# Rows 8 and 9 of the first chunk's down projection as three products each, with a reordered stage around them

## The chip, the cores and the metric

The kernel runs on one core of one Trainium2 chip. The metric is the time on the device in microseconds (us) of one execution, the median over runs. The engines of the core run beside each other, each through its own list of instructions in order: TensorE (PE; PEld is its loading of weights), VectorE (DVE), ScalarE (ACT), GpSimd (POOL) and SyncE (SP), which issues the DMAs. They wait for each other through semaphores.

## The reference

An mLSTM cell over 4 batches, 8 heads, 768 steps and head size 40, and then a two-layer network with exact GELU on its output, viewed as 3072 tokens by 320 features.

```python
for t in range(S):
    m_new = np.maximum(f_gate[:, :, t] + m, i_gate[:, :, t])
    f_stab = np.exp(f_gate[:, :, t] + m - m_new)
    i_stab = np.exp(i_gate[:, :, t] - m_new)
    m = m_new
    C = f_stab * C + i_stab * (v_t outer k_t)
    n = f_stab * n + i_stab * k_t
    y[:, :, t] = sigmoid(o_gate[:, :, t]) * (C @ q_t) / max(abs(n . q_t), 1)
x = y.transpose(0, 2, 1, 3).reshape(B * S, H * D)      # 3072 x 320
h = x @ w_in                                            # w_in 320 x 2048
out = (0.5 * h * (1 + erf(h / sqrt(2)))) @ w_out        # w_out 2048 x 320
```

All inputs are float32.

## The kernel before

**Chunks.** The 768 steps are cut into 6 chunks of 128. A chunk is computed in parallel form: scores of q and k within the chunk, weighted by the gates, and the carried state for what came earlier. Its y of all 4 batches (512 tokens) is transposed to x and goes through the two matrix products: "up" to 2048 features in 16 rows of 128 and GELU, then "down", where row n of the 16 adds its product with 128 rows of w_out into the four accumulators `po`, one for each batch.

**Products.** A float32 product on TensorE shows as two records in the profile. The alternative is three products in the type fp32r: one operand is split into a rounded part `hi`, a remainder `rest` and a rounded whole `low`, the other into `w_hi` and `w_lo`, and hi with w_hi, rest with w_hi and low with w_lo are added up (`w_parts` names them). Splitting a row of GELU's output is `split_g`: two instructions on ScalarE (hi at L873, low at L875) and one on VectorE (rest at L874). Splitting rows of w_out is `out_hi` (L935, on ScalarE for rows 8 and up) and `out_lo` (L943, VectorE). In the first chunk's down projection, rows 0 to 9 are fp32 and rows 10 to 15 are three products each (`row(n)`, L888).

**Weights.** w_in and w_out come in 26 pieces (0 to 9 of w_in, 10 to 25 of w_out, so that row n of the down projection needs piece 10 + n). Each is fetched as bits (L394, a ring of four buffers) and put together again by `conv_one` (two ScalarE instructions, L404 and L405, into one of two buffers `sig` and `pow`) and `conv_two` (two VectorE instructions, L416 and L419). `conv_two` of piece i also issues the fetch of piece i + 3, into the buffer that `conv_one` of piece i - 1 has read. `conv_one` of piece i needs the buffers that `conv_two` of piece i - 2 has left.

**The order.** The first part of the kernel (chunk 0, the cell of chunk 1, and all conversions) is written out by hand as the string `FRONT`. Each word is a step, and each engine gets its instructions in that order. The words that matter here:

- `K`, `J`: the next `conv_one`, `conv_two`; K22 is that of piece 22. `F`: the next row of the first down projection.
- `G`, `Y`, `X`, `R` of batch b, for chunk 1: tanh of the output gate (L506, ScalarE); `finish`, y from the values (L685 to L690, then `y_rest` at L699, VectorE); `turn_y`, y transposed on TensorE into the PSUM tile `px` (L708) and its rounded `x_hi` on ScalarE (L718); `split_x`, `x_rest` (L727) and `x_low` (L728) on VectorE. `V` are the cell's values.
- `z`: `split_g`. `a`, `b`: `out_hi`, `out_lo` of a row (a second number is how many rows).
- `r`, `p`: halves of the gate values out to DRAM and back, swapped; `+`: copies of k and q to a scratch in DRAM; `[`: blocks of that scratch loaded; `(`, `)`: the blocks turned on VectorE; `B`: a row of M broadcast (L210, L213). All but the turning are DMAs of SyncE.

For chunk 1, `px` has two buffers: batch 2's transposes take batch 0's, batch 3's take batch 1's, once their readers are done. In chunk 1 the steps X0 and X1 also issue the loads of k and v of chunk 2 for batches 0 and 1 (`load(n + NLD, 1, 3)`), ahead of the fetches of pieces 16 and 21 in SyncE's queue. Batches 1 and 3 of the chunks from 2 on are stored with their halves swapped, so that their loads are two DMAs each (L173).

After `FRONT` comes a second string for chunk 1's up and down projections (`SECOND`); it begins with the up projection `U0`, whose products are at L966.

Of the kernel before, what the change touches and what calls it, by code (L numbers as in the profile page):

```python
# [10 lines left out]
F32R = mybir.dt.float32r  # L11
# [3 lines left out]
OP = mybir.AluOpType  # L15

P = 128
# [10 lines left out]
    g1 c1 J y1 s2 K x0 t3 x1 v2 g2 O4 J B4 g3 c2 y2 s3 B5 K x2 K L5 J T0 K v3 A y3 M1 x3 c3 G0 M0 H O7 O6 O5 J  # L28
    J i5 u0 L6 u1 K W0 J W1 I4 A K S0 T1 C0 J i6 V0 i7 u2 G2 K U M2 L7 S1 J G1 K U i8 W2 J i9 C1 T2 K
    M3 f2 S2 V1 Y0 T3 J Y1 C2 e W3 K K K J S3 J C3 f3 K X0 J K R0 J K J V2 K Y2 J J K  # L30
    K V3 X1 J K r F J K (0 )0 F J K F K J F X2 G3 F J K F Y3 R1 J K F p + + + + J F J a10,2 b10,2 z10 a12 b12 F X3 z11 F a13,3 b13,3 z12 F z13 [1 F B8 z14 F B9 R2 z15 F R3 B10 B11 F a8 b8 a9 b9 F"""
CELL = "MWGVYXRKQDCSht"

HI_AT = {3: ("w_out3", 0), 8: ("w_out3", 2), 4: ("w_out0", 0), 5: ("w_out0", 1), 6: ("w_out2", 0), 7: ("w_out2", 1), 9: ("f0", 0)}
# [22 lines left out]
def kernel(  # L57
# [16 lines left out]
    nc = tc.nc  # L74

    B, H, S, D = q.shape
# [6 lines left out]
    DM = H * D  # L83
    DFF = moe_w_in.shape[1]
    NF = DFF // P
    TG = B * L
    R = P // 2
    NX = 2
    NLD = 4
# [11 lines left out]
    two = ctx.enter_context(tc.tile_pool(name="two", bufs=2))  # L101
# [5 lines left out]
    gp = ctx.enter_context(tc.tile_pool(name="gp", bufs=1))  # L107
# [25 lines left out]
    shared = lambda shape, dt, name: wts.tile(shape, dt, name=name, tag="hi", bufs=5)  # L133
# [16 lines left out]
    def out_of(n):  # L150
        return ob[n % NLD].rearrange("p (h d) -> p h d", d=D)
# [6 lines left out]
    def swapped(c, b):  # L158

        return c > 1 and b % 2 == 1  # L160

    def load(n, first=0, end=4):

        if n >= NCH * B:
            return
        c, b = divmod(n, B)
        for src, dst in ((q, qb), (k, kb), (v, vb), (o_gate, None))[first:end]:
            if dst is kb and c > 1:
                dst = k_later
            if dst and swapped(c, b):  # L170
                x, to = src[b, :, c * L:(c + 1) * L, :].rearrange("h p d -> p h d"), dst[turn_of(n)][:, :, 0:D]
                for i in range(2):
                    nc.sync.dma_start(out=to[halves[i]], in_=x[halves[1 - i]])  # L173
                continue
            nc.sync.dma_start(out=dst[turn_of(n)][:, :, 0:D] if dst else out_of(n),
                              in_=src[b, :, c * L:(c + 1) * L, :].rearrange("h p d -> p h d"))
# [19 lines left out]
    def turn_of(n):  # L196

        return n % NLD if n < 2 * B else (n - 2 * B) % NQ
# [36 lines left out]
    a = gates.tile([BH, NCH, L], F32, name="a")  # L235
# [141 lines left out]
    def w_row(n):  # L377

        return w_rows[n // 4][:, n % 4, :]
# [50 lines left out]
    def unread(bank):  # L430
        for _ in range(idle[0]):
            nc.tensor.matmul(bank, ident, ident, start=True, stop=True, skip_group_check=True)
        idle[0] = 0
# [8 lines left out]
    def by_set(px):  # L442

        return px.rearrange("p k (a i) -> p (k a) i", a=2)

    def in_place(x, b):

        return x.rearrange("p k (a t) -> p (k a) t", a=2)[:, :, b * R:(b + 1) * R]

    def in_turns(x):  # L450

        return x.rearrange("p (a t) -> p t a", a=2)

    def in_pairs(pu):

        return pu.rearrange("p (t a) -> p t a", a=2)

    class Cell:
# [242 lines left out]
        def turn_y(self, b):  # L701
            n, t = self.c * B + b, slice(b * L, (b + 1) * L)
            pool, tag = self.side[b // 2] if self.c > 1 else (ps_tr, "tr") if self.c > 0 else (ps_mm, "b")
            px = pool.tile([P, NX + 1, L], F32, name="px", tag=tag)
            unread(px[:, 0, :])
            for k in range(NX + 1):
                y = ob[n % NLD][:, k * P:(k + 1) * P] if k < NX else self.rest.get(b, y_rest).rearrange("p two r -> p (two r)")
                nc.tensor.transpose(px[:, k, :], y, ident)  # L708
            self.turned.append(b)
            if self.c < 2 and len(self.finished) > len(self.turned):  # L710
                self.twice(b + 1)
            if self.c == 0:
                nc.scalar.copy(out=first_x[:, :, t], in_=px)
                return
            self.px[b] = px
            if "x" not in parts:
                parts["x"] = raw.tile([P, NX + 1, TG], F32R, name="x_hi", tag="x", bufs=1)
            nc.scalar.activation(out=in_place(parts["x"], b), in_=by_set(px), func=AF.Copy, scale=PART)  # L718
            if self.c == 1 and b < 2:
                load(n + NLD, 1, 3)  # L720

        def split_x(self, b):
            px = by_set(self.px.pop(b))
            if b == 0:
                parts["x_low"] = fars[0].tile([P, NX + 1, TG], F32R, name="x_low", tag="x_low", bufs=1)
            hi = in_place(parts["x"], b)
            nc.vector.tensor_tensor(out=in_place(parts["x_rest"], b), in0=px, in1=hi, op=OP.subtract)  # L727
            nc.vector.tensor_copy(out=in_place(parts["x_low"], b), in_=px)  # L728


    HF, HT = NF // 2, TG // 2

    parts, fars, w_hi, w_lo, beside = {}, [], {}, {}, []
# [118 lines left out]
    def send(c, b, o_sb):  # L852
        to = out[b * S + c * L:b * S + (c + 1) * L, :]
        if c == 0:
            nc.sync.dma_start(out=to, in_=o_sb)
            return
        for a in range(2):
            queue = nc.scalar if a and c == NCH - 1 else nc.sync
            queue.dma_start(out=to[halves[a]], in_=o_sb[a::2])

    singles, first_parts_of = [], {}

    def split_g(n):

        parts_of = []
        for i in range(3 * len(first_parts_of), 3 * len(first_parts_of) + 3):
            if i == len(singles):
                four = gp.tile([P, 4, TG], F32R, name="g_part", tag=f"g{i // 4 % 3}")
                singles.extend(four[:, j, :] for j in range(4))
            parts_of.append(singles[i])  # L870
        hi, rest, low = first_parts_of[n] = parts_of
        whole = first_g.row(n)
        nc.scalar.activation(out=hi, in_=whole, func=AF.Copy, scale=PART)  # L873
        nc.vector.tensor_tensor(out=rest, in0=whole, in1=hi, op=OP.subtract)  # L874
        nc.scalar.copy(out=low, in_=whole)  # L875

    def first_down_steps(g):
        po = []

        def row(n):  # L880

            if n == 0:
                po.extend(ps_mm.tile([P, DM], F32, name="po", tag="ab"[b // 2]) for b in range(B))
            xs, ws = ((g.row(n),), (w_row(n),)) if n not in first_parts_of else (first_parts_of[n], later.w_parts(n))
            steps = [(k, b) for k in range(len(xs)) for b in range(B)]
            for k, b in sorted(steps, key=lambda x: x[::-1]) if n == NF - 1 else steps:
                to, w = (po[b], ws[k]) if len(xs) == 1 else (in_pairs(po[b]), in_turns(ws[k]))
                nc.tensor.matmul(to, xs[k][:, b * L:(b + 1) * L], w, start=(n == 0 and k == 0),  # L888
                                 stop=(n == NF - 1 and k + 1 == len(xs)), skip_group_check=True)
                if n == NF - 1 and k + 1 == len(xs):  # L890
                    if b % 2 == 0:
                        o_sb = outp.tile([P, 2, DM], F32, name="o_sb", tag="o_sb")
                    nc.scalar.activation(out=o_sb[:, b % 2, :].rearrange("p (a i) -> p a i", a=2),
                                         in_=po[b].rearrange("p (i a) -> p a i", a=2), func=AF.Copy)
                    send(0, b, o_sb[:, b % 2, :])

        return [lambda n=n: row(n) for n in range(NF)]
# [128 lines left out]
    def in_turn(steps):  # L1026
        todo = list(steps)
        return lambda: todo.pop(0)() if todo else None
# [9 lines left out]
    def first_blocks():  # L1038
# [3 lines left out]
        for r in (32, 96):  # L1042
# [3 lines left out]
    first_g, later = Hidden(), Later()  # L1046
# [5 lines left out]
                 A=in_turn(first_up_steps(0)), U=in_turn(first_up_steps(1)), e=first_blocks, F=in_turn(first_down_steps(first_g)),  # L1052
                 K=in_turn(lambda i=i: conv_one(i) for i in n_pieces), H=products_begin,
                 J=in_turn(lambda i=i: conv_two(i) for i in n_pieces), Z=split_weight,
                 u=first_parts, f=first_pair, i=split_first, z=split_g)
    steps |= dict(a=later.out_hi, b=later.out_lo)
    cell = cell_steps(2, CELL)
    steps |= {"+": copies, "<": cell["M"], ">": cell["W"], "(": cell["K"], ")": cell["Q"],
# [5 lines left out]
    for c in range(1, NCH):  # L1064
# [3 lines left out]
                     a=later.out_hi, b=later.out_lo, E=before and before.finish,  # L1068
                     L=lambda b: n0 + b < NCH * B and load_blocks(n0 + b, by_block), B=lambda b: load_M(n0 + b),
                     j=lambda b: load(n0 + b, 1, 3), o=lambda b: load(n0 + b, 3, 4), J=lambda b: load(n0 + b + NQ, 1, 3), O=lambda b: load(n0 + b + NLD, 3, 4))  # L1070
# [37 lines left out]
```

## Time and profile before

| | |
|---|---|
| median of 3 runs | 438.4 us (438.35 to 438.49) |
| the profiled execution | 438.46 us |
| its span | 436.7 us |
| TensorE busy | 427.3 us, 98% of the span |
| TensorE weight loads | 374.6 us, 86% |
| VectorE busy | 296.0 us, 68% |
| ScalarE busy | 277.3 us, 63% |
| GpSimd busy | 48.8 us, 11% |
| granted TensorE clock | 1.0 |

A timeline row gives the start in us, the time in us to the end of the group, engine, line, operation, output and input tiles, shapes and count; in brackets is how long the engine was idle before it and what ended that. A group's time runs to the end of its last instruction, and the next one often starts a little before that, so the step from one start to the next is what an instruction costs its engine. A row of the waits gives total us, number, and the longest. For DMA rows on SyncE (SPq) the time is that of the issue, with the wait for room in the queue.

### The profile page before, as it was taken

Reading aid. Unit: us, or ns where it says so; the run is one execution under the profiler, and the core shown is the slowest. Engines: PE = TensorE matmul, PEld = TensorE weight load, DVE = VectorE, ACT = ScalarE, POOL = GpSimd, SP = SyncE. Lnnn points to the kernel's source line nnn. Section 1 sums busy time; section 2 is a strip of 40 time slices with the busy share of each in tenths; the row PEclk is TensorE's granted clock in tenths of the full one; section 3 lists DMA queues with packets and bytes.
Section 4 is the critical chain, followed back from the end, with each engine's and each line's share of the span. In section 5 each row is a group of like instructions: output and inputs, shape, how many; then the busy total and the mean of one; then the engine's idle time right before and its main releaser. Section 6 shows DMA issues by size and latency. Waiting matters only on the chain.

```text
span 436.7 us, 13291 instructions
## 1 busy us (share of the span) xinstructions
PE 427.3 (98%) x5472; PEld 374.6 (86%) x5472; DVE 296.0 (68%) x680; ACT 277.3 (63%) x595; POOL 48.8 (11%) x77
## 2 busy tenths in 40 slices
PE   8989999999999999999999999999999999999996
PEld 7777888877988899988899988899988889979986
DVE  8797687797888697747597747597746586533330
ACT  4989999856889985228785229785247715243441
POOL 3001030000430041030041030040010000000000
PEclk9999999999999999999999999999999999999999
DMA  7999994577791592662492653571561400010001
GB/s 151 220 214 243 233 256 87 138 211 179 229 154 56 106 176 60 115 179 50 84 187 42 123 158 60 117 134 32 110 156 17 62 2 2 22 42 2 1 2 60
DMA packets 162268, 48.83 MB, mean 112 GB/s; under 512 B 147776, under 2 KB 155232, under 8 KB 162208
## 3 DMA queue, kind: packets, MB, share of 16 engines
q1 hardware_dynamic: 161888, 47.65, 50.1%
q8 instruction: 43, 0.70, 0.6%
q10 hardware_dynamic: 320, 0.33, 0.2%
q14 instruction: 17, 0.14, 0.1%
HBM read 43.84 MB, written 9.37 MB: 122 GB/s over the span
## 4 chain that ended last, share of the span: by engine, by line
PE 73%; DVE 2%; ACT 2%; DMA 1%; issue 1%; ACTq 0%
PE po L991 31%; PE pu L966 24%; PE pu L977 7%; PE ps L568 3%; PE pf L621 2%; PE ph L674 1%; PE po L888 1%; PE po L674 1%; PE px L708 1%; DMA bits<-in_moe_w_out_dram 1%; PE pf L632 1%; DVE pow L416 1%; DVE w_out L419 0%; ACT w_out_part L935 0%; ACT g_part L873 0%
## 5 line engine op out<-in xcount | busy, mean ns | idle before, releaser
L991 PE MATMUL po<-w_out_part,g_parts 128*128 128x320 f32 x960 | 140.7, 303 | 0.0
L991 PEld LDWEIGHTS po<-w_out_part,g_parts 128*128 128x128 f32 x960 | 131.6, 189 | 5.9 <-issue 4.6
L986 DVE TENSOR_TENSOR g_parts<-g_whole,g_parts 128x512 fp32r<-128x512 f32 x80 | 57.0, 713 | 58.1 <-ACT g_parts L985 56.0
L984 ACT ACTIVATE g_whole<-pu 128x512 f32<-128x512 f32 x80 | 47.1, 589 | 74.2 <-PE pu L977 63.7
L985 ACT ACTIVATE g_parts<-g_whole 128x512 fp32r<-128x512 f32 x80 | 50.5, 631 | 8.3 <-PE po L991 5.1
L474 POOL TENSOR_SCALAR_AFFINE_SELECT W<-W 128x1024 f32<-128x1024 f32 (+2 forms) x20 | 21.7, 1088 | 189.2 <-DMA W<-M_d 154.4
L500 ACT ACTIVATE W<-W,aT 128x128 f32<-128x128 f32 x128 | 38.8, 389 | 0.3
L987 DVE CAST g_parts<-g_whole 128x512 fp32r<-128x512 f32 x80 | 36.2, 453 | 0.0
L699 ACT COPY far<-ob 128x128 f32<-128x128 f32 x16 | 4.6, 290 | 32.9 <-DVE ob L690 32.9
L966 PE MATMUL pu<-x_hi,w_in_hi 128*128 128x512 f32 x80 | 24.2, 384 | 0.0
L966 PE MATMUL pu<-x_hi,hi_first 128*128 128x512 f32 x80 | 24.0, 381 | 0.1
L966 PE MATMUL pu<-x_rest,hi_first 128*128 128x512 f32 x80 | 23.8, 379 | 0.0
L966 PE MATMUL pu<-x_rest,w_in_hi 128*128 128x512 f32 x80 | 23.8, 379 | 0.0
L966 PE MATMUL pu<-x_low,w_in_lo 128*128 128x512 f32 x80 | 23.8, 379 | 0.0
L966 PE MATMUL pu<-x_low,w_in 128*128 128x512 f32 x80 | 23.8, 379 | 0.0
L888 PE MATMUL po<-w_out,g 128*128 128x320 f32 x80 | 22.0, 432 | 0.0
L404 ACT ACTIVATE sig<-bits 128x320 f32<-128x320 f32 (+1 forms) x26 | 15.2, 586 | 10.4 <-issue 6.1
L574 DVE TENSOR_TENSOR W<-ps,W 128x256 f32<-128x256 f32 (+1 forms) x48 | 17.7, 414 | 4.2 <-PE ps L568 3.2
L888 PEld LDWEIGHTS po<-w_out,g 128*128 128x128 f32 x80 | 15.0, 190 | 5.9
L639 DVE TENSOR_TENSOR far<-pf,gT 128x164 f32<-128x164 f32 x32 | 8.4, 319 | 16.1 <-PE pf L632 11.7
L416 DVE SCALAR_TENSOR_TENSOR pow<-sig,pow 128x320 uint32<-128x320 uint32 (+1 forms) x26 | 15.4, 592 | 4.3 <-ACT pow L405 4.3
L1015 ACT ACTIVATE o_sb<-po 128x320 f32<-128x320 f32 x20 | 7.5, 443 | 16.7 <-PE po L991 16.7
(196 smaller groups left out, 778.9 us busy)
## 6 DMA issues: line engine op xcount, KB each, us to landing
W<-M_d SPq DMA_DIRECT2D x16, 512.0 KB, 6.5
bits<-in_moe_w_in_dram SPq DMA_DIRECT2D x20, 256.0 KB, 4.2
bits<-in_moe_w_out_dram SPq DMA_DIRECT2D x16, 320.0 KB, 4.6
blocks<-kq_d SPq DMA_DIRECT2D x32, 128.0 KB, 3.5
ob<-in_o_gate_dram SPq DMA_DIRECT2D x24, 160.0 KB, 4.1
out_dram<-o_sb SPq DMA_DIRECT2D x36, 80.0 KB, 2.0
wide<-M_d SPq DMA_DIRECT2D x4, 512.0 KB, 4.8
kq_d<-in_k_dram SPq DMA_DIRECT2D x6, 320.0 KB, 4.6
```

The lines of the kernel that those rows point to most:

```text
L416: nc.vector.scalar_tensor_tensor(out=p, in0=s, scalar=3, in1=p, op0=OP.logical_shift_left, op1=OP.bitwise_or)
L474: nc.gpsimd.affine_select(out=x, in_=x, compare_op=OP.is_ge, fill=1.0e30, base=base, pattern=[[0, H], [1, x.shape[2]]], channel_multiplier=-1)
L500: nc.scalar.activation(out=W[n][:, h, :], in_=src, func=AF.Exp, scale=-1.0, bias=aT[:, self.c, r:r + 1])
L574: nc.vector.tensor_tensor(out=w[r, :, t], in0=ps[i][hip][r, :, t], in1=w[r, :, t], op=OP.mult)
L888: nc.tensor.matmul(to, xs[k][:, b * L:(b + 1) * L], w, start=(n == 0 and k == 0), stop=(n == NF - 1 and k + 1 == len(xs)), skip_group_chec ...
L966: nc.tensor.matmul(in_pairs(pus[i][e]), w3(at[k])[n][:, e, i * P:(i + 1) * P], in_turns(x3[n][:, k, :]), start=(n == 0 and k == 0), stop=F ...
L977: nc.tensor.matmul(in_pairs(pus[i][e]), w3(r)[n][h, p % 2, i * P:(i + 1) * P], in_turns(x3[n][h, NX, :]), start=False, stop=(n == 2), skip ...
L984: nc.scalar.activation(out=whole, in_=self.pus[n // 4][n % 4 // 2][n % 2], func=AF.Gelu)
L985: nc.scalar.activation(out=hi, in_=whole, func=AF.Copy, scale=PART)
L986: nc.vector.tensor_tensor(out=rest, in0=whole, in1=hi, op=OP.subtract)
L987: nc.vector.tensor_copy(out=low, in_=whole)
L991: nc.tensor.matmul(in_pairs(self.po[t]), x[:, t * L:(t + 1) * L], in_turns(w), start=(n == 0 and k == 0), stop=(n == NF - 1 and k == 2), s ...
```

## The change

- Rows 8 and 9 of the first down projection become three products too. Their parts of g lie in three tiles from the pool's "hi" buffers, their weights' parts in four tiles with the tags "vw", "vw", "kT" and "qT" (`first_homes`).
- `split_g` is cut in two: `z` keeps the two ScalarE instructions and the new `n` (`rest_g`) does the VectorE one. The split of the weights of rows 8 and 9 is two steps as well: `h` on ScalarE, `l` on VectorE (`split_row`).
- For chunk 1, `x_low` is made by ScalarE in `turn_y`, right behind `x_hi`, instead of by VectorE in `split_x`.
- The loads of k and v of chunk 2's batches 0 and 1 leave `turn_y` and become the steps `j0 j1`, behind row 12.
- The end of `FRONT` is put in a new order: among others X3, the fourth batch's transposes, stands ahead of row 8 instead of behind it, and the two splits of g for rows 8 and 9 ahead of K23 and X2.

```diff
-    K V3 X1 J K r F J K (0 )0 F J K F K J F X2 G3 F J K F Y3 R1 J K F p + + + + J F J a10,2 b10,2 z10 a12 b12 F X3 z11 F a13,3 b13,3 z12 F z13 [1 F B8 z14 F B9 R2 z15 F R3 B10 B11 F a8 b8 a9 b9 F"""
+    K V3 X1 J K r F J K (0 )0 F J K z8 F n8 F z9 K J X2 G3 n9 h8 F J l8 K h9 F Y3 R1 l9 z10 a10,2 J K F n10 b10,2 J F p + + + + X3 z11 J a12 n11 F b12 z12 F a13,3 n12 b13,3 F z13 n13 [1 F B8 z14 n14 F j0 j1 B9 R2 z15 n15 F R3 B10 B11 F a8 b8 a9 b9 F"""
...
             nc.scalar.activation(out=in_place(parts["x"], b), in_=by_set(px), func=AF.Copy, scale=PART)
-            if self.c == 1 and b < 2:
-                load(n + NLD, 1, 3)
+            if self.c == 1:
+                if b == 0:
+                    parts["x_low"] = fars[0].tile([P, NX + 1, TG], F32R, name="x_low", tag="x_low", bufs=1)
+                nc.scalar.copy(out=in_place(parts["x_low"], b), in_=by_set(px))
...
             nc.vector.tensor_tensor(out=in_place(parts["x_rest"], b), in0=px, in1=hi, op=OP.subtract)
-            nc.vector.tensor_copy(out=in_place(parts["x_low"], b), in_=px)
+            if self.c > 1:
+                nc.vector.tensor_copy(out=in_place(parts["x_low"], b), in_=px)
...
             if i == len(singles):
-                four = gp.tile([P, 4, TG], F32R, name="g_part", tag=f"g{i // 4 % 3}")
-                singles.extend(four[:, j, :] for j in range(4))
+                n_of, at = (2, 0) if i < 6 else (4, (i - 6) // 4 % 3)
+                t = shared([P, 2, TG], F32R, "g_part") if i < 6 else gp.tile([P, 4, TG], F32R, name="g_part", tag=f"g{at}")
+                singles.extend(t[:, j, :] for j in range(n_of))
...
         nc.scalar.activation(out=hi, in_=whole, func=AF.Copy, scale=PART)
-        nc.vector.tensor_tensor(out=rest, in0=whole, in1=hi, op=OP.subtract)
         nc.scalar.copy(out=low, in_=whole)
+
+    def rest_g(n):
+
+        hi, rest, low = first_parts_of[n]
+        nc.vector.tensor_tensor(out=rest, in0=first_g.row(n), in1=hi, op=OP.subtract)
+
+    first_homes, rows_lo = [], {}
+
+    def split_row(n):
+
+        to, lo = first_homes[2 * (n - HF):2 * (n - HF) + 2]
+        later.w_hi[n], later.w_lo[n] = to, lo
+        src, to, lo = [x.rearrange(f"p ({o}) -> p a t", a=2) for x, o in ((w_row(n), "t a"), (to, "a t"), (lo, "a t"))]
+        nc.scalar.copy(out=to, in_=src)
+        return lambda: nc.vector.tensor_tensor(out=lo, in0=src, in1=to, op=OP.subtract)
...
             if n == 0:
+                first_homes.extend(two.tile([P, DM], F32R, name="w_out_part", tag=tag) for tag in ("vw", "vw", "kT", "qT"))
...
-                 u=first_parts, f=first_pair, i=split_first, z=split_g)
+                 u=first_parts, f=first_pair, i=split_first, z=split_g, h=lambda n: rows_lo.update({n: split_row(n)}), l=lambda n: rows_lo.pop(n)(), n=rest_g, j=lambda b: load(2 * B + b, 1, 3))
```

More of the change, by code (lines that the diff above doesn't have):

```diff
@@ L718, in turn_y @@
             nc.scalar.activation(out=in_place(parts["x"], b), in_=by_set(px), func=AF.Copy, scale=PART)
-            if self.c == 1 and b < 2:
-                load(n + NLD, 1, 3)
+            if self.c == 1:
+                if b == 0:
+                    parts["x_low"] = fars[0].tile([P, NX + 1, TG], F32R, name="x_low", tag="x_low", bufs=1)
+                nc.scalar.copy(out=in_place(parts["x_low"], b), in_=by_set(px))
         def split_x(self, b):
             px = by_set(self.px.pop(b))
-            if b == 0:
+            if b == 0 and self.c > 1:
                 parts["x_low"] = fars[0].tile([P, NX + 1, TG], F32R, name="x_low", tag="x_low", bufs=1)
```

## The prediction

> **What bounds the kernel now.** I read the page first (TensorE busy for 427.3 us of a 436.7 us span), then the waits of TensorE, then the timeline of each engine over 84 to 119 us, where the first chunk's down projection and the second chunk's x are made. The waits of TensorE between 80 and 170 us are one line:
>
> ```profile
> PE po L888 <- DVE g_part L874: 0.6, 2, 0.4
> ```
>
> After 118.69 us, where the second chunk's up projection starts, TensorE idles under 0.5 us, so a shift of that start is a shift of the end. TensorE's timeline of the stage:
>
> ```profile
> 85.53 8.78 PE L888 MATMUL po<-w_out,g 128*128 128x320 f32 x32
> 94.15 0.38 PE L708 MATMUL px<-ident,ob 128*128 128x128 f32 x2
> ...
> 94.47 10.93 PE L888 MATMUL po<-w_out,g 128*128 128x320 f32 x40
> 105.24 0.38 PE L708 MATMUL px<-ident,ob 128*128 128x128 f32 x2
> ...
> 105.57 2.32 PE L888 MATMUL po<-w_out,g 128*128 128x320 f32 x8
> 107.50 0.93 PE L888 MATMUL po<-w_out_part,g_part 128*128 128x320 f32 x4
> 108.70 3.53 PE L888 MATMUL po<-w_out_part,g_part 128*128 128x320 f32 x24 [0.27 <-DVE g_part L874]
> 112.61 6.24 PE L888 MATMUL po<-w_out_part,g_part 128*128 128x320 f32 x44 [0.38 <-DVE g_part L874]
> ```
>
> Four fp32 rows take 94.15 - 85.53 = 8.62, so 2.155 a row. The last 44 products take 118.69 - 112.61 = 6.08, so 0.138 each and 1.66 for a row of 12. Rows 10 to 15 should take 72 x 0.138 = 9.95 and take 118.69 - 107.50 = 11.19: 1.24 us of stall, for splits that come late. The px transposes (0.33 with what follows) never wait.
>
> VectorE's timeline: batch 0's x_rest, conversion 21's first half, Y3, and R1 behind it.
>
> ```profile
> 85.99 0.56 DVE L727 TENSOR_TENSOR x_rest<-px,x_hi 128x384 fp32r<-128x384 f32 x1 [1.07 <-ACT x_hi L718]
> 97.17 0.48 DVE L416 SCALAR_TENSOR_TENSOR pow<-sig,pow 128x320 uint32<-128x320 uint32 x1
> 101.45 0.49 DVE L685 SCALAR_TENSOR_TENSOR ob<-ob,far 128x320 f32<-128x320 f32 x1 [0.58 <-ACT ob L506]
> 103.23 0.55 DVE L727 TENSOR_TENSOR x_rest<-px,x_hi 128x384 fp32r<-128x384 f32 x1
> ```
>
> ScalarE's timeline: it waits for the bits of piece 22 (K22), then come the third batch's x_hi, the tanh of G3 that Y3 waits for, and at 106.83 row 10's split, needed at 107.50.
>
> ```profile
> 98.85 0.49 ACT L404 ACTIVATE sig<-bits 128x320 f32<-128x320 f32 x1 [1.99 <-DMA bits<-in_moe_w_out_dram]
> 100.59 0.47 ACT L718 ACTIVATE x_hi<-px 128x384 fp32r<-128x384 f32 x1
> 100.96 0.46 ACT L506 ACTIVATE ob<-ob 128x320 f32<-128x320 f32 x1
> 106.83 0.63 ACT L873 ACTIVATE g_part<-g 128x512 fp32r<-128x512 f32 x1
> ```
>
> SyncE's own queue: four k and v DMAs stand ahead of the bits of piece 21.
>
> ```profile
> 89.42 1.34 SPq L173 DMA_DIRECT2D wide<-in_k_dram  x2
> 90.86 1.27 SPq L173 DMA_DIRECT2D vb<-in_v_dram  x2
> 92.23 0.56 SPq L394 DMA_DIRECT2D bits<-in_moe_w_out_dram  x1
> ```
>
> **Part by part.** *Two rows as three products:* 2 x (2.155 - 1.66) = 0.99 us less on TensorE. The price is off it: on ScalarE four g_part operations (1.04 a row, from 108.74 to 109.77) and two weight copies (0.39); on VectorE two subtractions of 0.60 and two of 0.41. If no split came late the 1.24 of stall would go too.
>
> *x_low on ScalarE:* VectorE loses 0.47 four times (103.23 to 103.70), ScalarE gains 0.37 four times (x_hi's step, 100.59 to 100.96, the same shape). Both engines now read one px. The trace shows no two of its readers at once (x_hi, then x_rest, then x_low, each after the other); so batch 0's x_rest waits between 0 and the copy's 0.35. I take 0.35, the value by the rows, all of which stand one behind another.
>
> [...]
>
> *k and v out of the bits' queue:* SyncE issued six DMAs at the first two transposes; the four at 89.42 held piece 21 until 92.23, and the two at 78.75 held nothing that VectorE did not hold longer. Piece 22 is issued once conversion 18 has left its buffer: K18 starts 0.08 after VectorE's step 16, which moves from 90.78 to 90.66, ends 91.68, so K18 ends 92.73 and the fetch goes at 92.8. Its landing took 4.9 in the crowded queue, others 2.9 to 3.3 (issued at 78.4 and 89.0) and 4.5 (86.8). I take up to 4.4, landed by 97.2. The six DMAs now stand behind the blocks' loads and ahead of three M loads: some 3.7 us of SP issue (0.43 + 0.59, and 2.8 for the halves) ahead of B9, B10, B11. The second of these masks (L474) ran from 115.46 to 117.66 on POOL; ScalarE's weights of that batch follow 2.4 us behind 120.64, and the weighed values that POOL makes behind it (to 119.3) are read at 126.53 (L632). SP's queue runs 1 us earlier in front of them, so all this comes some 3 us later than now, to 120.7 and 122.3: still 2.3 and 4.2 us early. Uncovered, each us beyond that is a us of time. The two "vw" and one each of the "kT" and "qT" buffers that rows 8 and 9 borrow were read last by 85 us and are next written after 115 us; the same holds for the three borrowed "hi" buffers. Cost nothing.
>
> *The moved order, which decides.* The fourth px transpose goes from behind row 8 to ahead of it. It needs the second px's buffer, so batch 1's x_rest (Y3, then R1 on VectorE) must be done. TensorE is there at 85.53 + 8 x 2.155 + 0.33 = 103.1. When is R1 done? ScalarE's new copies and the two g splits now stand ahead of G3, and G3 ahead of Y3 and R1:
>
> - x_hi at 85.46, x_low to 86.31, R0 at 86.34. From R0 to the end of conversion 20, VectorE worked without a gap, 85.99 to 97.26 = 11.27; less x_low 0.47 it is 10.80: 97.14.
> - K22 needs that buffer: 97.22 (0.08, as from 87.94 to 88.02). Its bits are there. K takes 0.87; row 8's hi starts 98.09 and ends (0.62) 98.71.
> - Row 8's subtraction is now ahead of J21: 98.74 + 0.60, J21 from 99.34 to 100.36. K23 waits for J21's buffer: 100.44 (both g splits lie within that wait).
> - K23 0.87, x_hi 0.37, x_low 0.37: the tanh at 102.05, done 102.51; the weight copy of row 8 behind it 102.41 to 102.90.
> - On VectorE row 8's weight rest waits for it: 102.93 + 0.41; Y3 at 103.34, y_rest 1.64 later, R1 at 105.12 to 105.67.
> - px at 105.73, row 8 at 106.06.
>
> So TensorE waits 2.6 us at the transpose. Behind it the splits are early: row 11's rest is needed at 111.6 and done at 110.84, row 13's at 114.9 and done 114.2. No stall is left there. Eight rows of 12 x 0.138 = 13.27 end at 119.33 against 118.69: +0.64.
>
> The sum: 2.64 of new wait - 0.99 of products - 1.24 of old stall, and 0.23 in which the first product of row 10 now overlaps the last fp32 pass: +0.64. The profiled execution took 438.46 (span 436.7 and 1.8 around it), 0.06 over the median of 438.4: 439.1.
>
> **The rivals.** *No wait at the transpose (faster).* If R1 is done by 103.1, row 8 starts at 103.42 and the eight rows end at 116.69: -2.0, 436.5. For it: ScalarE has idle stretches of 2.0 and 3.0 us before 98.85 and 105.26 that the splits could fill, and VectorE is relieved. Against: filling them needs K22 and K23 2.6 us earlier, and VectorE's unbroken work from 86 us holds them. Every us by which G3 is earlier than 102.05 is a us of time; 438.75 needs only that the reads of px overlap.
>
> *Late bits (slower).* The fetch of piece 22 at 92.8 lands after 97.2, and K22, the splits, G3, Y3, R1 and the px slide with it one for one. With the 4.9 and 5.2 that the pieces issued at 93.85, 94.4 and 95.3 took it is at 97.7 to 98.0: 0.5 to 0.8 more, 439.6 to 439.9; I take 439.8. It decides slower from a landing over 4.6. For it: the halves of aT and ewT are still written through the same queue just ahead. Against: the four k and v DMAs are gone.
>
> *The move of k and v does nothing:* without those DMAs K22 is held by conversion 20 at nearly the same time, so in the forecast that part gives only what x_low and the splits take. It is in the sum.
>
> **How the numbers follow.** A measurement here tells 0.2% (0.9 us) from no change: 437.5 to 439.3. The forecast, a wait that eats the saving, has 0.58, its own range 438.6 to 439.6; 0.47 of that lies below 439.3 and 0.11 above. Late bits 0.27, no wait 0.15. So faster 0.15, same 0.47, slower 0.38. The range goes from 437.3, where 1.8 of the 2.6 us of wait are gone (G3 can come earlier by any part of it), to 440.0, the late bits' upper end: it leaves out 0.14 below and some 0.05 above.
>
> **What would show it.** Right: TensorE's row L708 with an idle of 2 to 3 us before it near 105.7, ended by VectorE's x_rest; L888 as 96 split products without an idle; K22 released by VectorE, not by a DMA; the up projection's first product near 119.3. Wrong: the transpose near 103 us without idle and the up projection near 117; or K22 ended by its DMA later than 97.4; or waits behind 120 us at the values (L632) or weights (L500) for the moved loads.

## The result and the profile after

The changed kernel took 439.97 us (median of 8 runs, 438.72 to 440.46) against 438.3 us (8 runs): a ratio of 1.0039, 95% interval 1.0027 to 1.0051. It is slower by 0.4%, about 1.7 us. The profiled execution took 439.94 us with a span of 438.1. The forecast was 439.1 and "no change that can be measured"; the time lies just under the upper end of the range, 440.0, and above the 439.3 up to which the forecast counted as no change.

TensorE's timeline of the stage, changed kernel (start, length, line, tiles; idle before it and what ended that in brackets):

```profile
85.45 8.78 PE L907 MATMUL po<-w_out,g 128*128 128x320 f32 x32
...
105.81 0.41 PE L708 MATMUL px<-ident,ob 128*128 128x128 f32 x2 [2.64 <-DVE x_rest L729]
...
106.08 14.96 PE L907 MATMUL po<-w_out_part,g_part 128*128 128x320 f32 x96
120.88 0.59 PE L985 MATMUL pu<-x_hi,hi_first 128*128 128x512 f32 x2
```

The fourth px waits 2.64 us for batch 1's x_rest; the forecast had 2.6 us at 105.73. Behind it the 96 split products (three for each fp32 product of rows 8 to 15) run without an idle, as forecast, but take 120.88 - 106.08 = 14.80 us and not 13.27. Busy times by stretch show why (columns: stretch, length, then busy time and count for TensorE, its weight loads, VectorE, ScalarE and POOL, then granted clock, DMA share and GB/s):

```profile
107.20:110.60 3.40, 3.40 (x15) 3.40 (x14) 3.33 (x7) 3.40 (x8) 0.00 (x0) 0.50 0.90 155
110.60:121.00 10.40, 10.40 (x78) 10.40 (x77) 9.61 (x15) 6.98 (x14) 3.21 (x4) 1.00 0.81 231
```

From 107.2 to 110.6 the granted clock is 0.50. TensorE is busy all of that time and does 15 products where full clock does some 25 (3.40 / 0.138). The page shows it as a single 8 in the row PEclk and nowhere else; a busy share of 98% hides it.

I call the time from row 0 of the down projection to the second chunk's up projection "the stage". It took 33.16 us before (118.69 - 85.53) and 35.43 after (120.88 - 85.45). That is +2.27 where +0.64 was worked out. The span grew by only 1.4: behind the stage the rest took 318.0 before and 317.2 after. Over all profiles of this study that rest lies between 317.1 and 318.0, and row 0 starts between 85.4 and 87.2. The two profiles of the old order have 318.0 and 317.9, those of the changed kernel and its variants 317.1 to 318.0; whether an edit moves the rest is not shown. So the stage measures the part that was edited, and the ratio of times judges the whole.

### The profile page after: what moved, and what is told of

The parts are those of the page before. It is cut to its first block, busy times and chain, and to the rows that moved or that the text cites. A ratio compares the mean times of both kernels' runs of the same rounds, so it can differ in the third digit from the quotient of the medians.

```text
span 438.1 us, 13313 instructions
## 1 busy us (share of the span) xinstructions
PE 427.8 (98%) x5480; PEld 376.6 (86%) x5480; DVE 295.6 (67%) x680; ACT 281.8 (64%) x605; POOL 48.4 (11%) x77
## 4 chain that ended last, share of the span: by engine, by line
PE 75%; DVE 1%; ACT 0%; issue 0%; DVEq 0%
PE po L1010 31%; PE pu L985 24%; PE pu L996 7%; PE po L907 3%; PE ps L568 3%; PE pf L621 2%; PE ph L674 1%; PE px L708 1%; PE po L674 1%; PE pf L632 1%; DVE ob L690 0%; DVE w_out_part L893 0%; DVE x_rest L729 0%; ACT o_sb L1034 0%; DVE ob L685 0%
## 5 line engine op out<-in xcount | busy, mean ns | idle before, releaser
L1005 DVE TENSOR_TENSOR g_parts<-g_whole,g_parts 128x512 fp32r<-128x512 f32 x80 | 57.9, 724 | 58.9 <-ACT g_parts L1004 56.7
L474 POOL TENSOR_SCALAR_AFFINE_SELECT W<-W 128x1024 f32<-128x1024 f32 (+2 forms) x20 | 20.3, 1018 | 193.9 <-DMA W<-M_d 117.3
L512 DVE STREAM_TRANSPOSE kT<-blocks 128x512 f32<-128x512 f32 x16 | 11.3, 709 | 12.3 <-DMA blocks<-kq_d 12.2
L907 PE MATMUL po<-w_out,g 128*128 128x320 f32 x64 | 17.6, 432 | 0.0
L405 ACT ACTIVATE pow<-bits,low_bits 128x320 uint32<-128x320 uint32 (+1 forms) x26 | 17.4, 669 | 0.0
```

The costliest lines, as they stand in the source:

```text
L405: nc.scalar.activation(out=p, in_=lo, func=AF.Relu, scale=0.9 * 2.0 ** -29, bias=low_bits)
L474: nc.gpsimd.affine_select(out=x, in_=x, compare_op=OP.is_ge, fill=1.0e30, base=base, pattern=[[0, H], [1, x.shape[2]]], channel_multiplier=-1)
```

## The experiments

The theory after this had two parts. **Wait theory:** the transposes moved ahead of row 8 wait for R1, which the reordered ScalarE and VectorE work makes late. **Clock theory:** the idle stretch itself halves the clock for 3.4 us and costs 1.5 more. Rivals: the added ScalarE work as such, the moved loads, the reads of px on two engines.

**Splits moved into an idle stretch of ScalarE.**

```diff
-... K J V2 K Y2 J J K
-... F J K z8 F n8 F z9 K J X2 G3 ...
+... K J V2 K z8 z9 Y2 J J K
+... F J K F n8 F K J X2 G3 ...
```

> The changed kernel with one move: the ScalarE halves of the two g splits of rows 8 and 9 stand ahead of K18, in a stretch of 1.9 us in which ScalarE idles, instead of ahead of K23. Same work, same products. Wait theory (the loss is TensorE's wait at the fourth px for batch 1's x_rest, and half a clock behind it): K23, G3, Y3 and R1 come about 1.7 us earlier, the wait falls from 2.6 to about 0.9 us, the granted clock stays 1.0, the second chunk's up projection starts near 117.5 instead of 120.9, and the time is 2.5 to 3.5 us under the changed kernel's, about 1 us under the kernel before. Work theory (the added ScalarE work itself makes the stage longer): the same work in the same stage, the up projection stays near 120 to 121 and the time within 0.5 us of the changed kernel's.

TensorE's timeline with the early splits:

```profile
86.38 8.78 PE L907 MATMUL po<-w_out,g 128*128 128x320 f32 x32
...
105.00 0.41 PE L708 MATMUL px<-ident,ob 128*128 128x128 f32 x2 [0.90 <-DVE x_rest L729]
...
105.27 13.29 PE L907 MATMUL po<-w_out_part,g_part 128*128 128x320 f32 x96
118.40 0.59 PE L985 MATMUL pu<-x_hi,hi_first 128*128 128x512 f32 x2
```

The wait is 0.90, the products take 13.13, the stage 118.40 - 86.38 = 32.02 (row 0 starts 0.9 later in this execution, so 117.5 became 118.4). The ratio to the kernel before is 0.9963 (0.9946 to 0.9980). The same work in another place turns slower into faster: the added ScalarE work as such is not the cost.

**The gap filled with products of no use.**

```diff
-... p + + + + X3 z11 ...
+... p + + + + k10 X3 z11 ...
```

> The changed kernel with ten products of no use (128x128 fp32, some 0.24 us each) on TensorE between row 7 and the fourth px: they fill 2.4 of the 2.6 us of wait and change nothing else. Clock theory (the idle stretch itself makes the clock fall to half for 3.4 us, worth 1.5 us): the transposes still come near 105.8, the granted clock is 1.0 throughout, the 96 split products take 13.3 instead of 14.8 us, the up projection starts near 119.4, and the time is about 1.5 us under the changed kernel's. Rival (the products of rows 8 to 15 run slower for another reason, as DMA or operand reads beside them, and the clock's row only goes along): the 96 products still take about 14.8 and the time stays.

TensorE's timeline with the ten fillers:

```profile
85.47 8.78 PE L907 MATMUL po<-w_out,g 128*128 128x320 f32 x32
...
103.03 2.39 PE L250 MATMUL cold<-w_out 128*128 128x128 f32 x20
105.81 0.41 PE L708 MATMUL px<-ident,ob 128*128 128x128 f32 x2 [0.39 <-DVE x_rest L729]
...
106.08 8.94 PE L907 MATMUL po<-w_out_part,g_part 128*128 128x320 f32 x64
115.23 4.61 PE L907 MATMUL po<-w_out_part,g_part 128*128 128x320 f32 x32 [0.21 <-DVE g_part L883]
119.68 0.59 PE L985 MATMUL pu<-x_hi,hi_first 128*128 128x512 f32 x2
```

The transposes come at the same 105.81, the granted clock of the profiled execution is 1.0, and the products end at 119.68 instead of 120.88. The 1.5 us expected is 1.2, because at full clock row 13's rest comes late: the products take 119.68 - 106.08 = 13.60 us, against 13.13 with the early splits. Ratio 1.0015 (0.9996 to 1.0034), no different from the kernel before. This interval overlaps that of the changed kernel, so the gain rests on the trace (a stage of 34.21 instead of 35.43) and on the clock, 0.999 or more in all 12 runs. With useless work in the gap the clock stayed up: the clock theory holds.

**The transposes moved alone, in the kernel before.**

```diff
-... z10 a12 b12 F X3 z11 F a13,3 ...
+... z10 a12 b12 X3 F z11 F a13,3 ...
```

> The kernel before with one move: the fourth px transposes ahead of row 8 instead of behind it. Wait theory: batch 1's split of x ends at 104.3 there and TensorE is at 103.1, so a wait of about 1.3 us at the transposes, ended by VectorE; it takes the place of the 1.2 us of stall at rows 10 to 12, so the up projection starts within 0.4 us of before and the time is the same within 0.5 us; a gap this short leaves the clock at 1.0. If the place of the transposes alone made the loss, the time would rise by 1.3 us or more.

```profile
105.48 0.41 PE L708 MATMUL px<-ident,ob 128*128 128x128 f32 x2 [0.76 <-DVE x_low L728]
```

That line of its TensorE timeline is the wait: 0.76 us, shorter than the 1.3 expected. The stage is 32.93, the ratio 1.0002 (0.9983 to 1.0021). The new place costs nothing by itself; it only makes R1 decisive.

**The loads of k and v back in the bits' queue.**

```diff
+                if b < 2:
+                    load(n + NLD, 1, 3)
...
-... F j0 j1 B9 R2 ...
+... F B9 R2 ...
```

> The changed kernel with the loads of k and v of chunk 2's batches 0 and 1 back at the second chunk's first two transposes. Wait theory: the bits of piece 22 land near 98.7 instead of before 97.2, everything behind K22 slides, and the wait at the fourth px grows from 2.6 to about 4.1 us: 1.0 to 2.0 us slower than the changed kernel. If the moved loads themselves cost the loss (M's masks behind them, late k and v): faster than the changed kernel by up to 1.5 us.

```profile
98.80 0.49 ACT L404 ACTIVATE sig<-bits 128x320 f32<-128x320 f32 x1 [0.41 <-DMA bits<-in_moe_w_out_dram]
```

In its ScalarE timeline K22 is again released by the bits, at 98.80; in the changed kernel it starts at 97.20. TensorE waits 3.74 us at the fourth px (4.1 expected, 2.64 in the changed kernel), the clock is at half for 6.83 us, the stage takes 37.64. Ratio 1.0061 (1.0032 to 1.0090), 1.0 us over the changed kernel by the ratios, whose intervals overlap; the trace is what shows it. So the moved loads were a gain in this order, and not the loss.

**x_low back on VectorE.** The edit undoes that part of the change in `turn_y` and `split_x`.

> The changed kernel with x_low back on VectorE, all else as changed. Wait theory: ScalarE's chain to G3 is shorter by one copy (0.37), batch 0's x_rest no longer waits 0.35, but VectorE has 0.47 more in batch 0 and 0.47 more ahead of the release of the second px: the wait at the fourth px is 2.7 to 2.9 instead of 2.6 us, the stage within 0.4 us of the changed kernel's, so this part is worth next to nothing either way. If the wait of VectorE for ScalarE's reads of px were what costs, the stage would be 0.5 us or more shorter.

The wait is 2.81 us, ended by x_low on VectorE; ratio 1.0033 (1.0018 to 1.0049). As expected, worth next to nothing. Its profiled execution kept the clock at 1.00 from 104.0 to 120.4 and had a stage of 34.10, while 6 of its 12 runs show a mean granted clock of 0.996 or less: with the same edit the clock fell in some executions only. (A fall of 3.41 us to half takes 0.5 x 3.41 / 438, so 0.004, off the mean. Of the runs of the kernel before that were timed beside the variants, none shows a mean under 0.998.)

**The changed kernel again.**

> The changed kernel unchanged, on the same chip as its variants. A wait of 2.6 us at the fourth px again, ended by VectorE's x_rest; from row 0 to the up projection 33.9 us where the clock stays at 1.0 and about 35.4 where it falls to half for 3.4 us. Time 1.003 to 1.005 of the kernel before.

Wait 2.62, stage 35.42, half clock for 3.41 us; ratio 1.0036 (1.0017 to 1.0054). Of the 12 runs 5 show a clock of 0.996 or less and average 441.5 us, the 7 others average 440.2: 1.3 us for the clock. Of the first eight runs 3 show a clock of 0.996 or less, and there the difference is only 0.3 us (440.0 and 439.7).

**How much idle stood ahead of a fall.** In the traces of the two kernels each record of the granted clock that ends within the trace lasts a whole multiple of 3.413 us: in the changed kernel 102.400 at full clock (30 steps), 3.413 at half and 327.679 at full (96 steps), in the kernel before 433.493 at full (127 steps). The steps so laid out are the grid here. Its step just before each fall held 2.02 us of idle (changed kernel), 2.06 (the same kernel run again) and 2.60 (loads back), and with x_low back a step with 2.00 brought no fall. The ends of the two kernels agree: the step in which the last product ends held 0.45 us of idle in the changed kernel and 1.58 in the kernel before, and no fall followed in either; behind the next one, idle for all of its 3.41 us, the clock fell in both. Two more fillings of the gap test that.

```diff
-... p + + + + X3 z11 ...
+... p + + + + k4 X3 z11 ...      (and k1 in the other)
```

> The changed kernel with four products of no use at the start of the gap instead of ten: 0.95 of the 2.64 us are filled and about 1.7 us of TensorE stay idle. In the traces so far the clock fell to half for the next 3.41 us where one stretch of a fixed grid of 3.41 us held 2.02, 2.06 or 2.60 us of idle, and did not where it held 2.00 or less. Grid theory: no stretch can hold over 1.7, so the granted clock stays at 1.0 (0.998 or more over the run) in every run, the 96 products take 13.3 us in each, and the time is that of the kernel with ten fillers, about 1 us under the changed kernel. Rival (any wait of TensorE beyond a us puts the clock at risk): some of the runs show 0.996 or less.

> The same with one product of no use: 0.24 us filled, 2.4 us idle. Grid theory: a stretch of 3.41 us holds over 2.03 of these 2.4 in (3.41 + 2.4 - 4.06) / 3.41 = 51% of its positions, so some half of the runs show 0.996 or less and half 0.998 or more, as in the changed kernel (58% by the same sum with 2.64), and the time is the changed kernel's within 0.5 us. Rival (only the length of the gap decides, with a limit between 1.7 and 2.6 us): all runs alike.

Their lines of the TensorE timeline, four fillers first:

```profile
106.53 0.41 PE L708 MATMUL px<-ident,ob 128*128 128x128 f32 x2 [1.71 <-DVE x_rest L729]
```

```profile
107.52 0.41 PE L708 MATMUL px<-ident,ob 128*128 128x128 f32 x2 [2.38 <-DVE x_rest L729]
```

With 1.71 us idle none of 11 runs shows a clock under 0.998; the stage is 34.06 and the ratio 1.0025 (1.0011 to 1.0040). With 2.38 idle 7 of 12 show 0.996 or less, the profiled one among them, stage 35.40; ratio 1.0033 (1.0017 to 1.0049). Neither all nor none, as the grid theory expected and its rival did not. Its shares are not confirmed: with 2.62 to 2.64 us idle it expects 58% and 8 of 20 runs fell, which so few runs cannot settle. The time with four fillers was expected to equal that with ten; it is 0.0010 above in ratio, within the intervals.

**An order without the wait.** On top of the early splits, VectorE's rests of g and w_out for rows 8 and 9 move behind R1 where TensorE does not need them yet.

```diff
-... J K F n8 F K J X2 G3 n9 h8 F J l8 K h9 F Y3 R1 l9 z10 ...
+... J K F F K J X2 G3 n8 h8 F J K h9 F Y3 R1 n9 l8 l9 z10 ...
```

> The changed kernel in an order worked out from the traces' own durations: the ScalarE halves of the g splits ahead of K18, X2 and G3 straight behind K23, and on VectorE the rests of g and of w_out of rows 8 and 9 moved so that G3, Y3 and R1 are never behind them. Same work. Wait theory: R1 is done at about 102.5, ahead of TensorE at 103.1; no wait at the fourth px, granted clock 1.0, from row 0 to the second chunk's up projection 31.1 us (33.2 before, 35.4 in the changed kernel, 32.0 with the first move alone), and the time is about 2 us (0.5%) under the kernel before, 3.5 to 4.3 under the changed one. Rival (something behind this stage, such as M's masks behind the moved loads, takes over): the stage shrinks but waits appear behind 117 us, and the time is no lower than with the first move alone.

Its TensorE timeline:

```profile
86.33 8.78 PE L907 MATMUL po<-w_out,g 128*128 128x320 f32 x32
...
103.88 0.38 PE L708 MATMUL px<-ident,ob 128*128 128x128 f32 x2
...
104.13 13.64 PE L907 MATMUL po<-w_out_part,g_part 128*128 128x320 f32 x96
117.60 0.59 PE L985 MATMUL pu<-x_hi,hi_first 128*128 128x512 f32 x2
```

No wait at the transposes, a granted clock of 0.999 over the profiled execution, a stage of 31.27, and TensorE shows no wait behind it either. Ratio 0.9965 (0.9952 to 0.9978): it beats the kernel before by 1.5 us and the changed one by about 3. The 2 us expected is not reached, and by time it cannot be told from the first move alone, though its stage is 0.75 shorter.

**The same order with rows 8 and 9 in fp32.** All `z`, `n`, `h`, `l` of rows 8 and 9 are left out of the string.

> The same order without the three products: rows 8 and 9 are fp32 again, the eight splits for them left out, everything else as in the order without a wait (the loads moved, x_low on ScalarE, rests of g as steps). It measures the products alone. Both theories: no wait at the fourth px. By the price of the rows (2.155 against 1.66 a row) the stage takes 32.1 us, 1.0 longer than with three products and 1.1 shorter than before, because the late splits' stall is gone; time 0.9 to 1.1 us under the kernel before. Rival (the products gain nothing of their own, only the order does): the same time as with the three products, within 0.3 us of stage.

Stage 31.98, ratio 0.9975 (0.9963 to 0.9988). So the order with the moved loads and x_low is worth 1.2 us of stage without any new product, and the three products of rows 8 and 9 are worth 31.98 - 31.27 = 0.71 where this run was expected to show 1.0; their own gain in time lies within the intervals.

## Why the prediction was right or wrong

**The moved order: right, step by step.** The chain was worked out from rows of before, and each step lies within 0.1 us of the changed kernel's trace. VectorE's timeline after:

```profile
86.28 0.56 DVE L729 TENSOR_TENSOR x_rest<-px,x_hi 128x384 fp32r<-128x384 f32 x1 [1.44 <-ACT x_low L722]
...
102.93 0.49 DVE L893 TENSOR_TENSOR w_out_part<-w_out,w_out_part 128x320 fp32r<-128x320 f32 x1 [1.04 <-ACT w_out_part L892]
103.34 0.48 DVE L685 SCALAR_TENSOR_TENSOR ob<-ob,far 128x320 f32<-128x320 f32 x1
...
105.11 0.55 DVE L729 TENSOR_TENSOR x_rest<-px,x_hi 128x384 fp32r<-128x384 f32 x1
```

R0 was expected at 86.34, row 8's rest at 98.74 (it came at 98.72), its weight rest at 102.93, Y3 at 103.34, R1 at 105.12. The first line also settles the two reads of one px: x_rest is released by ScalarE's x_low (85.74, 0.51 us), not by x_hi (85.37, 0.51 us), and starts at 86.28, so the 0.35 taken was there, and the 438.75 of reads that overlap (439.1 less 0.35) did not come about.

ScalarE's timeline after, K22 and K23:

```profile
97.20 0.49 ACT L404 ACTIVATE sig<-bits 128x320 f32<-128x320 f32 x1 [1.07 <-issue]
...
100.43 0.51 ACT L404 ACTIVATE sig<-bits 128x320 f32<-128x320 f32 x1 [0.19 <-ACT g_part L878]
```

K22 was expected at 97.22, released by VectorE: VectorE's conversion 20 ended at 97.12 and no DMA is named here, so the rival of late bits did not come about. K23 was expected at 100.44.

**The moved loads: right.** The second mask ran to 120.54 on POOL (120.7 expected) and the weighed values to 123.1 (122.3 expected). ScalarE's weights of that batch start at 122.83, without a wait for the mask, and TensorE reads the weighed values at 128.72; neither waited.

**The three products: right in size, in part by luck.** 0.99 us was expected of them, less the 0.23 by which the old order overlaps the first split product with the last fp32 pass, so 0.76; measured in an order without a wait it is 0.71. But a row costs less than the 1.66 us taken, since 96 products need 13.13 and not 13.27 us with the early splits; and the order without a wait still loses 0.34 to late splits (117.60 - 104.13 = 13.47).

**What failed: the step "eight rows of 12 x 0.138 = 13.27 end at 119.33".** It carried the full-clock price of a product across a gap of 2.6 us. The term left out is the clock: 14.80 - 13.27 = 1.53 us in the executions where it falls, 8 of the changed kernel's 20. With it the sum is 0.64 + 1.53 = 2.17 against 2.27 measured for the stage. Between its first and its last product the kernel before never shows TensorE idle for more than 1.1 us at a time, and its clock is 1.0 from its first record at 4.45 us on, so the rows of its stage held no price for this. (Only its very start shows slower products: the slowest of L250 takes 579 ns and starts before 4.4 us, and those from there on have a median of 275.) The prediction named no price of its own: neither a rival nor the range contained a clock that falls. It had the wait's place and its size right and stopped at its end.

**The step "no stall is left there" failed too, where the clock held.** It had row 13's rest needed at 114.9 and done at 114.2. Ahead of it on VectorE stands the subtraction for the weights of rows 13 to 15. Before:

```profile
110.79 1.16 DVE L943 TENSOR_TENSOR w_out_part<-w_out,w_out_part 128x960 fp32r<-128x960 f32 x1 [0.81 <-ACT w_out_part L935]
```

After, with a mask of POOL beside its start:

```profile
112.42 1.09 POOL L474 TENSOR_SCALAR_AFFINE_SELECT W<-W 128x1024 f32<-128x1024 f32 x1 [48.20 <-DMA W<-M_d]
112.58 1.94 DVE L962 TENSOR_TENSOR w_out_part<-w_out,w_out_part 128x960 fp32r<-128x960 f32 x1 [0.76 <-ACT w_out_part L954]
```

Row 13's rest follows it at 114.44 and is done at 115.1. At half clock TensorE comes there later and does not wait. At full clock it does: the products take 13.60 us with ten fillers, 13.46 with four and 13.30 with x_low back, so up to 0.33 over the 13.27 of the sum. Without a fall of the clock that makes up to 0.64 + 0.33 = 0.97, and these three variants, whose profiles kept the clock, show 1.05, 0.90 and 0.94 (stages of 34.21, 34.06 and 34.10).

**What stays open.** Both steps are read from stages of traces. By time, the changed kernel is above the 0.7 us of the forecast even where the clock held: 1.6 us over the mean of the kernel before in 5 of the first eight runs and 1.1 in 7 of the twelve repeated ones. Where it fell it is 1.9 (3 runs) and 2.4 us (5 runs). So the clock explains the profiled execution and only a part of the median; the late row 13 is worth up to 0.3 more, and what is left of the first runs' 1.6 was not traced to a row. The eight runs of the kernel before alone spread over 1.5 us. That 439.97 still lies inside the range is luck: its upper end was worked out for late bits, which did not come.

**The chances.** "No change" at 0.47 rested on the wait eating the saving almost exactly. Of the chance of 0.38 for slower, 0.27 was put on late bits, which did not come, and 0.11 on the forecast's own spread; the clock, which did come, had no share of it.

## What to carry to other kernels

When an edit makes the busiest engine wait, price what runs behind the wait anew and don't take it from rows at full clock: here, with a wait of TensorE of 2.38 to 2.81 us in the profiled execution, the clock fell to half in 21 of 44 runs, and three traces with a fall show 1.5 us more for the products behind it (14.80 and not 13.27). If the wait can't be removed, filling it with products of no use kept the clock at 0.999 or more here (ten products, 12 runs). And before adding work to the engine that feeds the bottleneck, look for a stretch in which it idles anyway: moving two splits from ahead of K23 to ahead of K18 took 1.7 us off the wait here.

## What the runs showed of the hardware

- In the traces of the two kernels the records of the granted clock last whole multiples of 3.413 us: 30, 1 and 96 in the changed kernel, 127 in the kernel before. From full clock, a step of 3.413 us with 2.02, 2.06 or 2.60 us of TensorE idle (changed kernel, run again, loads back) was followed by half clock for 3.41 us, and one with 2.00 (x_low back) or 1.58 (the end of the kernel before) was not; with the loads back, 2.60 and then 1.14 in two steps in a row gave 6.83 us. By runs, with the gap of the profiled execution: a mean clock of 0.996 or less in none of 11 with 1.71, 7 of 12 with 2.38, 8 of 20 with 2.62 to 2.64, 6 of 12 with 2.81.
- The subtraction on VectorE of 128x960 ahead of row 13 took 1.16 us where no mask of POOL (L474, 128x1024, 1.09 us) was running at its start: in the kernel before, in the order without a wait and in that order with rows 8 and 9 in fp32. It took 1.94, 2.02, 1.88 and 1.67 where 0.93, 1.00, 0.87 and 0.66 us of a mask were still to come (changed kernel, ten fillers, four fillers, x_low back), so 0.51 to 0.86 more, each time 0.14 or 0.15 less than what was left of the mask; why is not shown.
